# A planned kernel with the orders of its engines exchanged: recurrent attention into a two-expert layer

## The chip, the cores and the metric

One core of a Trainium2 chip runs the program. The metric is the device time of one execution in microseconds; with several runs, their median.

## The reference

The first half is a recurrence over 768 steps for 4 batches of 8 heads of 40 dimensions. Each head keeps a 40x40 state C, a vector n and a maximum m:

```python
m_new = np.maximum(f + m, i)
f_stab, i_stab = np.exp(f + m - m_new), np.exp(i - m_new)
C = f_stab * C + i_stab * np.einsum('bhd,bhe->bhde', vt, kt)
n = f_stab * n + i_stab * kt
y = sigmoid(o_gate) * (C q) / np.maximum(np.abs(n . q), 1.0)
```

Its output, 3072 rows of 320 numbers, goes into a layer of 8 experts with top-1 choice: the logits are `x @ w_gate + modality_bias[modality_id]`, the chosen expert computes `relu(x @ w1[e]) @ w2[e]` (320 to 1024 and back to 320), scaled by the softmax weight of the choice.

## The kernel before, in words

Two parts run interleaved on one core. The **attention part** treats 24 chunks of 128 rows. The first 22 use states that change little (light chunks): states of the first batches are made from k, v and gate weights (`states`, L1890 to L1937), then each light chunk is one product of q with the state. Chunks 0 to 9 take it in full precision (L2042), chunks 10 to 21 as a product of a high and a low half in half precision (L2056); the split of q is done by ACT (the high half, L2049) and DVE (the low half, L2050). The last two chunks of work are special passes with scores (L2146) and values (L2161), for which POOL adds a mask to a sum of gates and takes an offset off (L2150, L2152). After a pair of chunks, `token_rows` divides and gates the rows (DVE L2071 to L2078), POOL or DVE multiplies (L2084, L2086, L2094), ACT rounds to half precision (L2087, L2096), DVE makes the low half (L2089, L2098), and POOL scatters the rows to a table in DRAM, sorted by modality (L2105). A sigmoid of the gates is ACT's L2022; ACT's L2023 is a check of them whose sum (`junk`) is read by the verdict at the end alone.

The **expert part** has 14 tiles of rows, eight for expert A and six for expert B (the stream is A0, A1, A2, B0, B1, A3, ...). For the first three tiles rows are selected on PE by products with selection matrices (L2232 to L2239) and copied by ACT (L2245 to L2249); later ones are loaded from the table (L2200). ACT copies the third part of a tile's columns to where PE needs them in two steps (L2323, L2324: `xt<-xt`). Logits are PE's L2272 and DVE's L2277 to L2293. The first layer is PE's L2344 with its tails L2352, ACT and DVE split the result into two halves (`hh` L2332, `hl` L2333), the second layer is PE's L2403 in groups of four products, ACT scales (L2416) and POOL scatters the result (L2418). Expert weights are loaded in eight pieces for each expert through staging tiles; ACT (L2015) and DVE (L2016) split each piece. One row that fits no tile (`odd_row`) is computed on DVE, with two products on PE (L2443, L2475).

The **order** isn't written in the code as it reads. `still_arm` adds 1126 steps to a `Plan`, each with its engine, an estimated duration and its dependencies. `Plan.run` takes a text, `ORDER` (L1595), two characters for each step, and splits it into one sequence for each engine: 305 steps of PE, 443 of DVE, 200 of ACT, 79 of POOL and 99 of SP, which issues transfers. It walks the sequences by the plan's own estimates to one order in which all instructions are emitted; every engine then runs its own in that order. Three things are derived from the planned times: `gaps` puts fill matmuls of zeros (L2602) into planned gaps of PE in the first 60 us; a GpSimd transfer is made to wait for the DVE step planned ahead of it; and a GpSimd product for the last DVE step of the kind that works within SBUF alone:

```python
flat = [k[a] * len(self.DIGITS) + k[b] for a, b in zip(text[::2], text[1::2])]
...
self.seq = {e: [i for i in flat if ts[i]["eng"] == e] for e in self.ENGINES}
...
order = plan.run(ORDER)
fills = plan.gaps(["M0", "O1", "O0", "Y0", "Y1", "H0", "H1", "H2"], 0.25, 60.0, "zz")
```

Of the kernel before, what the change touches and what calls it, by code (L numbers as in the profile page):

```python
# [1594 lines left out]
ORDER = (  # L1595
    "#:#;#7#W#X#Y$($'$>$=$z$y$L&3&4$N$P&K&L$T$b$c$e%k%l%m%n%,%o%-$h%/%1%t%u%v%w%x%}%~%5'6&#&$&%&&&i&j&k&n&o&r&s&v&w&z&{&|&}&~"
    "'#'(')'*'+','-%^(;(<(=(@(A(D'Q&/'N(E(H(I(L(M(N(O(P(Q(T(U(V(W'v(X(Y'y&[).)/)0)3)4)7)8);)<(i(l)?)@)A)B)C)D)G)H)I)J)K)L'b*4"
    ")V*5*6*9*:)Y*=*>*A)o*B*E)r*F*G*H*I*J*M*N*O*P*Q*R*g*h(,+4*i*l*m*p*q,9*t*u*x+7({*y*z*{*|,>,C*}+$+%+&+'+(+),H*%+W+X+[*W+_+b"
    "+e+f+i+l+o+r+s+t+u+v+w+z+{+|+}+~,#,&,',(,),*,+,.,/,0+F,1,X,2,3,y,z,}-$-'-*,h-+-.-1-Z-4-7-8-9-:-;-<-?-@-A-B-C-D-G-H-I-J-K"
    '-L-O-P-Q-R-S-T.B.C.F.I-r.L.O.P.S.V.Y.].^._.`.a.b.e.f.g.h.i.j.m.n.o.p.q.r.u.v.w.x.y.z/$/%/&/)/*/-/./1/2/5/6/7/8.7/9/:/=/>'  # L1600
    "/?/@/A/B.<#)#|#}#*#+#<#.#9#2#1#3#F#4#=#K#?#>#N#A#G#@#B#T#U'H#H#V#Z#[#I#]#C#D#J$O%0%.#L$&$*$d$.$K#M$)$-$+$,$@$/$D$?$C$A$1"
    "$B$2%$${%#$|$5$}$M$6$G$~$H#R&9&5&:$R&6&7#d&F$U#g%'$f&8%(#s&R#j%q#m&N$V%3$i&M#p'5$W&Q#v#y$X%s%|%z'8$Z&O$[$_'M$`$]$j$k$l%6"
    "%7#6$a&=&>%8&P%N&q&u&m&y$r$s%9&U&V%E%H%?%K%@$n'%%A%;$o%W$p'>$t%_%`'P%Z%a(?%Q'S'R'V%b'T$q'U$^%T'W(C(G(K'u'Z%h'[&0'x%i%j(h"
    "'z&]&^%d%<%=%e%>'~&_&`%f'{'|(#&b'}%g)2(k):)6&f(m'G)>(n(o(&&g&h(')U(r)X(q(p)Z'c)_)n'd(u(v)`'e)[)]'f)^)q*@*8'l*<*D)c)d)t&c"
    "&d&e+3)s)w'h'm'n)x)u)v+<+8){)|'i'j(-(.'k(/*k+6*o(0,=+=(|+9(}(~*w+:)#)%+;)&*s(2,G(6)'(3(7,I(8,J,K,M)(*&,L)))*+@+A*',N+Z(4"
    '*X)++a+^*(*)*+,Q*,*Y*Z,R+h+d*/+k+n(5*0*1+q(b+G+H+I*[,|-#+J-&*^,Y%+*-+L*.,Z,i*_*`,[,]*b*c*a,_,`,a-)*d-[,b-3---0,c,j+M-6,k'
    ",l+N+O-](c-^'_+P+Q+R-_-a,d(d,n,o-b-c(e)g,r,e-e,p'I-l-m'J'K,s,t-n,U-h-i-f-g-o-p-q.E-s-{-d.K-v.H,q-t-u.R(f.N-w-x.U.[.$.X-j"
    ".%.&.'.(.).*.+.,-k.-.:-y-z.../.0.1.2.3.4.5/,.6/0.;/(/4.=###5#S$%#z#8#E#^#_#`$;&E$0$4$w$F&+#c$Q$S#f%&#r$g&C#i%p#l#o%2#u%r"
    "%4#x%{%y'7$Y'L#{&<%M&'&p$m&l&t%D&x&T%V%G%J%:'$'O$<(9(:'=$x%Y'&(>'.%P'3(B%S%c&,(F(J't'Y'w(g&D'4),(R)-'r's(Z)1(j)5)9(%(`&a"
    ")=)T,<)W*2)R)E*3)m(t)k)M*7)p*;*?*C'g)b,7+2+0*f*e*K)z*j(a+5+S*n*r*S#(+T*v,F(1*~+V+?)$+U+Y)S+*+]+`+c**,P+g+j+m+p+x,x,$,,.>"  # L1610
    ",u,w,v,~,{)l-%,4*]+1-(,8.A+K-/,^.?-,-2-5-=-`.@-E,m.~-M.D-U.J.G.M.Q.T.W.Z.c/#.k.s.{/'/+///3.8/;/C#/#,#~#-#P#O#0$3$E%%$I$8"
    "#Q$7%)$J&;%*&?&S&@&W&X&1&('X''']'^,:'/($,;(S((()(s([(w)a(x)f)e)y)F)})N,D,E+>*L*T+B,O)~+C,S+#,T+y++,-,%+,,5->-V-|-F-N.d.l"
    ".t.|-W.}.9/</D#$#%#&#'$9$:$u$v$#&)&*#a#b&A$$#e#q&B#h#k#n#t&-#w&G'0%B%F%L%I%C%U'9'1%[&H&I%X%O'2':';&.'<&J%R'o'p'E(]&Y%]'q"
    "'F'?(^)O(_)P'A)Q'@'`)h'B,A&Z)j'C)i,6+/+-+.(*,B'D(y(+'a,?,@*#(z*U&2+E+D,V,W,f-X*V-Y,g*$-}-~.#"
)
SMALL = dict(tok=NC, u=NC, lo=NC, hi=NC, mod=NC, u25=NHALF, erev=E, mb=NMOD * E, wg=3 * E, tok2=6, cmask=FT)

# [1141 lines left out]
```

## Time and profile before

| | |
|---|---|
| median of 3 runs | 205.23 us (205.13 to 205.27) |
| profiled execution, its own time | 207.16 us |
| its span, first to last instruction | 205.4 us |
| mean granted clock of PE | 0.99 |
| HBM read, written | 23.13 MB, 8.75 MB |

A row of a timeline tells start, duration, engine, line, operation, output and inputs, shape and count (consecutive alike instructions are one row), and in brackets how long the engine had been idle and what released it. PE's rows overlap, since its matmuls are pipelined: what one costs is read from the start of the next.

### The profile page before, as it was taken

How to read it: one execution, taken by the hardware profiler on the slowest of the kernel's cores; microseconds unless marked ns; L12 is line 12 of the kernel's file. 1: busy time of each engine (PE TensorE's matmuls, PEld its weight loads, DVE VectorE, ACT ScalarE, POOL GpSimd, SP SyncE). 2: the span in 40 equal slices, each digit the busy share in tenths (PEclk: the TensorE clock that was granted, in tenths of full speed). 3: DMA queues.
4: the chain of work that ended last, by engine and by line, in shares of the span. 5: the costliest groups of instructions: out<-in, count | busy, mean ns of one | idle time of the engine just before them, and what ended most of it. 6: DMA issues, size and time to landing. Idle time of an engine off the chain costs nothing.

```text
span 205.4 us, 4934 instructions
## 1 busy us (share of the span) xinstructions
PE 195.7 (95%) x1850; PEld 136.0 (66%) x1850; DVE 136.1 (66%) x451; ACT 108.4 (53%) x212; POOL 83.0 (40%) x85
## 2 busy tenths in 40 slices
...
GB/s 182 370 330 392 369 398 220 306 327 238 319 345 260 311 386 190 134 68 176 103 52 99 79 150 190 6 0 32 35 64 0 33 112 389 142 64 20 2 40 34
DMA packets 29548, 35.77 MB, mean 174 GB/s; under 512 B 19421, under 2 KB 21151, under 8 KB 29263
## 3 DMA queue, kind: packets, MB, share of 16 engines
...
q0 software_dynamic: 2416, 8.13, 11.6%
q8 instruction: 15, 0.25, 0.5%
...
HBM read 23.13 MB, written 8.75 MB: 155 GB/s over the span
## 4 chain that ended last, share of the span: by engine, by line
PE 80%; DVE 8%; ACT 4%; issue 3%; POOL 1%; POOLq 0%; ACTq 0%
PE O L2403 35%; PE H L2344 20%; PE H L2352 7%; PE O L2344 6%; PE M L2272 2%; PE M L2602 2%; DVE qst L2050 1%; PE Y L2056 1%; DVE xr L2078 1%; PE Y L2161 1%; PE Y L2146 1%; PE O L2232 1%; ACT qst L2049 1%; ACT junk L2023 1%; PE Y L2042 1%
## 5 line engine op out<-in xcount | busy, mean ns | idle before, releaser
L2418 POOL DMA_INDIRECT out<-ob,ois x25 | 28.2, 1129 | 59.4 <-ACT ob L2416 19.3
L2403 PEld LDWEIGHTS <-hh 128*128 128x128 f16 (+1 forms) x400 | 37.7, 98 | 15.4 <-issue 0.4
L2105 POOL DMA_INDIRECT x_s<-rows,pos_i x24 | 28.5, 1186 | 26.0 <-issue 6.8
L2333 DVE SCALAR_TENSOR_TENSOR hl<-H,hh 128x512 f16<-128x512 f32 (+2 forms) x40 | 25.0, 646 | 18.1 <-ACT hh L2332 17.7
L2332 ACT ACTIVATE hh<-H 128x512 f16<-128x512 f32 (+2 forms) x40 | 22.0, 563 | 28.0 <-PE H L2344 15.9
L2416 ACT ACTIVATE ob<-O,zs 128x320 f32<-128x320 f32 x24 | 12.6, 524 | 30.1 <-PE O L2403 20.7
L2403 PE MATMUL O<-w2hA,hh 128*128 128x320 f16 (+1 forms) x104 | 27.8, 299 | 0.0
L2403 PE MATMUL O<-w2lA,hh 128*128 128x320 f16 (+1 forms) x104 | 27.8, 299 | 0.0
L2403 PE MATMUL O<-w2hB,hh 128*128 128x320 f16 x96 | 26.5, 299 | 0.0
L2403 PE MATMUL O<-w2lB,hh 128*128 128x320 f16 x96 | 26.5, 299 | 0.0
L2344 PE MATMUL H<-xt,w1hA 128*128 128x512 f16 (+3 forms) x128 | 24.5, 295 | 0.0
L2403 PEld LDWEIGHTS <-hl 128*128 128x128 f16 (+1 forms) x200 | 18.9, 98 | 7.8 <-issue 0.7
L2344 PE MATMUL H<-xt,w1hB 128*128 128x256 f16 (+1 forms) x120 | 23.4, 294 | 0.0
L2344 PEld LDWEIGHTS <-w1hA 128*128 128x128 f16 x160 | 13.7, 98 | 8.3 <-issue 2.1
L2344 PEld LDWEIGHTS <-w1hB 128*128 128x128 f16 x160 | 14.8, 98 | 6.2 <-issue 1.9
L2344 PE MATMUL H<-xt,w1lA 128*128 128x512 f16 (+3 forms) x64 | 18.1, 294 | 0.0
L2344 PE MATMUL H<-xt,w1lB 128*128 128x256 f16 (+1 forms) x60 | 17.6, 294 | 0.0
L2094 POOL TENSOR_TENSOR xr<-xr,ab 128x640 f32<-128x640 f32 x11 | 14.0, 1272 | 5.1 <-DVE rows L2098 1.9
L2403 PE MATMUL O<-w2hA,hl 128*128 128x320 f16 (+1 forms) x104 | 15.7, 299 | 0.0
L2050 DVE SCALAR_TENSOR_TENSOR qst<-qg,qst 40x1024 f16<-40x1024 f32 x12 | 15.3, 1271 | 0.3 <-ACT qst L2049 0.3
L2403 PE MATMUL O<-w2hB,hl 128*128 128x320 f16 x96 | 15.2, 299 | 0.0
L2078 DVE SCALAR_TENSOR_TENSOR xr<-og,Y 128x320 f32<-128x320 f32 x24 | 11.5, 479 | 5.3 <-ACT rows L2096 2.5
...
## 6 DMA issues: line engine op xcount, KB each, us to landing
...
```

Source lines behind the costliest of these rows:

```text
L2050: two(H * P, lambda: v.scalar_tensor_tensor(qst[j][0:D], qf[j][0:D], QSC, qst[j][0:D], ALU.mult, ALU.subtract), r=[f"qf{j}"], w=[f"qh{j}"])
L2078: dve(320, lambda h=h: v.scalar_tensor_tensor(x4[:, h], og[k][:, h].rearrange("p (h d) -> p h d", h=H), 1.0, y4[h][:, :, 0:D], ALU.add, AL ...
L2094: on(640, lambda: by.tensor_tensor(x3, x3, ab.rearrange("p c h o -> p (c h) o").broadcast_to([P, 2 * H, D]), ALU.mult), r=abk, w=xk)
L2105: ins = g_.indirect_dma_start(out=x_s[:, :], out_offset=bass.IndirectOffsetOnAxis(ap=pos_i[:, c:c + 1].bitcast(U32), axis=0), in_=rows[:, ...
L2272: t_.matmul(M0[0:n, 16 * h:16 * h + 16], lhsT=s["x"][:, b, P * h:P * h + n], rhs=wgr[:, b % 3].rearrange("p a e -> p (a e)"), start=(h == ...
L2332: act(len(f) * n, lambda: s_.activation(hh[:, sl, 0:n], hp3, AF.Relu), r=[nb], w=[f"hh{p}"])
L2333: dve(len(f) * n, lambda: v.scalar_tensor_tensor(hl[:, sl, 0:n], hp3, 0.0, hh[:, sl, 0:n], ALU.max, ALU.subtract), r=[nb, f"hh{p}"], w=[f" ...
L2344: t_.matmul(dst, lhsT=w[:, i, ws], rhs=two_x(xb), start=(first and b == 0 and q == 0), stop=(last and b == 1 and q == 2), skip_group_check ...
L2352: t_.matmul(dst, lhsT=w[rs, place(f)[0], 2 * T:WP], rhs=two_x(xs[r], rs), start=(f in fresh and q == 0), stop=(f in last and q == 2), skip ...
L2403: t_.matmul(op[p0:p0 + nr, 0:DM], lhsT=t[:, at[f], o_:o_ + nr], rhs=w[:, f], start=(i < ways), stop=(i >= 24 - ways), skip_group_check=True)
L2416: act(DM + 80, lambda op=op, o=o, qc=qc, nr=nr: s_.mul(obs[o][0:nr], op[0:nr, 0:DM], facs[0:nr, qc:qc + 1]), r=[no, f"fac{m_}"], w=[f"ob{o}"])
L2418: swdma(164, lambda o=o, qc=qc, nr=nr: disjoint("outf", g_.indirect_dma_start(out=out[:, :], out_offset=bass.IndirectOffsetOnAxis(ap=ois[0 ...
```

## The change

Only the text `ORDER` is replaced. The steps, their instructions, their dependencies and all the code stay. Since the five sequences are other ones, so are the one order in which instructions are emitted, the fills, and the DVE steps for which POOL's transfers and products wait.

```diff
@@ -1593,25 +1593,25 @@
 ORDER = (
-    "#:#;#7#W#X#Y$($'$>$=$z$y$L&3&4$N$P&K&L$T$b$c$e%k%l%m%n%,%o%-$h%/%1%t%u%v%w%x%}%~%5'6&#&$&%&&&i&j&k&n&o&r&s&v&w&z&{&|&}&~"
-    "'#'(')'*'+','-%^(;(<(=(@(A(D'Q&/'N(E(H(I(L(M(N(O(P(Q(T(U(V(W'v(X(Y'y&[).)/)0)3)4)7)8);)<(i(l)?)@)A)B)C)D)G)H)I)J)K)L'b*4"
-    ")V*5*6*9*:)Y*=*>*A)o*B*E)r*F*G*H*I*J*M*N*O*P*Q*R*g*h(,+4*i*l*m*p*q,9*t*u*x+7({*y*z*{*|,>,C*}+$+%+&+'+(+),H*%+W+X+[*W+_+b"
...
-    ".t.|-W.}.9/</D#$#%#&#'$9$:$u$v$#&)&*#a#b&A$$#e#q&B#h#k#n#t&-#w&G'0%B%F%L%I%C%U'9'1%[&H&I%X%O'2':';&.'<&J%R'o'p'E(]&Y%]'q"
-    "'F'?(^)O(_)P'A)Q'@'`)h'B,A&Z)j'C)i,6+/+-+.(*,B'D(y(+'a,?,@*#(z*U&2+E+D,V,W,f-X*V-Y,g*$-}-~.#"
+    "#:#;#7#W#X#Y$($'$>$=$z$y&4&3$L$N$P&L&K$b$c$e$T%k%l%m%n%o%,%-%/%1$h%t%u%v%w%x%}%~&#'6%5&$&%&&&i&j&k&n&o&r&s&v&w&z&{&|&}&~"
+    "'#'(')'*'+','-%^(;(<(=(@(A(D'N'Q(E(H(I(L(M(N(O'v&/(P(Q(T(U(V(W(X(Y'y&[).)/)0)3)4)7(l)8(i);)<)?)@)A)B)C)D)G)H)I)J)V)Y)K)L"
+    "'b*4*5*6*9*:*=*>)r*A)o*B*E*F*G*H*I*J*M*N*O*P*Q*R(,*g*h*i*l*m*p*q+7*t+4*u({,9*x*y,>*z*{*|*}+$+%+&+',C+(+),H*%+W+X+[*W+_+b"
...
+    ".d.}.t.9.|/</D#$#%$##&#'$9$:$u$v&)$$&*&A#a#e#b#n#h#k&-#q#t&B&G#w%B'0%F%C%I%X'9'1%L%[%R%U&I%O&H&J'<':';'2'o'p(]%]&Y'?(^&."
+    "'q)O'B'A(_)P'@)Q)h&Z'`'E)i'C'F)j+/'a+-,6(*'D,A+.&2(z(y,B,@,?*#*U(+*$+D,g*V,V+E-Y-X,W,f-}-~.#"
 )
```

Decoded, the fewest steps that have to be taken out and put back to turn one sequence into the other are 28 of PE's 305, 235 of DVE's 443, 97 of ACT's 200, 31 of POOL's 79 and 45 of SP's 99. The fills (columns of zeros) become:

| ahead of | before | after |
|---|---|---|
| the counts, L1950 | 2699 | 3444 |
| the turn of the gate weights, L1879 | 1135 | 818 |
| the first states, L1911 | 772 | 772 |
| light chunk 1 | 836 | 808 |
| light chunk 3 | 364 | 251 |
| light chunk 5 | 1163 | 2319 |
| light chunks 6 and 7 | 1394 | 260 |
| select of tile 0, chunk 2 | 0 | 332 |
| logits of tile 0 | 0 | 302 |

The moves that the text below speaks of (places in the sequence of the step's own engine):

| engine | step | move |
|---|---|---|
| PE | light chunks 7 and 6, L2042 | ahead of all selects of tile 0, 7 before 6 |
| PE | light chunk 9 before 8; logits of tile 0 | logits behind the selects of tile 1 |
| PE | values of light chunk 12, L2056 | 7 places earlier |
| PE | values of chunks 15, 14, L2056 | 4 and 1 earlier, into the first layer of tile 4, 15 first |
| PE | values of chunks 16, 17, 19, 21 | 4, 8, 4, 5 earlier |
| PE | values of chunk 20; special scores and values, pair 0; scores, pair 1 | 7 later; 4 later and 3 earlier; 5 later |
| DVE | low state half, L1937 | 32 earlier, behind the rows of pair 0 |
| DVE | low half of q, L2050, of chunk 14 | 8 later, next ahead of the logits of tile 4 |
| DVE | L2050 of chunks 15, 16, 17 | 3 earlier, 8 earlier, 2 later |
| ACT | checks L2023 of pairs 0, 1 | 30 and 41 earlier |
| ACT | split of piece 0 of A's weights, L2015; pieces 1 and 4 | 4 later; 1 and 6 earlier; now 1, 0, 4 |
| ACT | last copy of tile 0, L2249 | 4 later, behind those three splits |
| ACT | rounding of pair 4, L2096 | 6 earlier |
| ACT | copies of tile 3, L2323, L2324; split of piece 6 of B | 2 and 3 later; 13 later, behind the copies |
| ACT | high half of q, L2049, of chunk 11, of chunk 15 | 7 later, behind the copies; 5 earlier |
| POOL | product of pair 4, L2094 | ahead of the scatter of chunk 6 |
| POOL | special mask sum L2150, pair 0 | 8 later |
| SP | store of zero rows, L2121 | 6 earlier, ahead of the first loads of q and the gates |
| SP | loads of A's pieces 0, 1 and 4 | 3 later, 1 and 4 earlier: now 1, 0, 4 |
| SP | loads of q of chunks 14, 15 | 2 and 4 earlier |

## Rows read from the trace of the kernel before

**Rows 1.** The page, part 1: busy time of each engine.

```profile
PE 195.7 (95%) x1850; PEld 136.0 (66%) x1850; DVE 136.1 (66%) x451; ACT 108.4 (53%) x212; POOL 83.0 (40%) x85
```

**Rows 2.** The page, part 4: the chain that ended last, shares by engine.

```profile
PE 80%; DVE 8%; ACT 4%; issue 3%; POOL 1%; POOLq 0%; ACTq 0%
```

**Rows 3.** The table of stages: length, then PE, PEld, DVE, ACT, POOL busy; clock, DMA share, GB/s.

```profile
10.00:20.00 10.00, 9.87 (x124) 8.43 (x123) 9.39 (x38) 7.31 (x14) 5.20 (x5) 1.00 1.01 361
...
100.00:150.00 50.00, 50.00 (x390) 28.42 (x388) 26.89 (x88) 21.77 (x49) 15.01 (x16) 1.00 0.28 67
```

**Rows 4.** PE's waits: who waited for whom, in total, times, longest.

```profile
PE Y L2056 <- DVE qst L2050: 0.6, 1, 0.6
```

**Rows 5.** Timeline of PE, the start: start, duration, line, operation, count.

```profile
1.07 2.43 PE L2602 MATMUL M<-zz 128*128 128x512 bf16 x6 [1.07 <-DVE zz L1832]
...
10.91 0.66 PE L2602 MATMUL M<-zz 128*128 128x512 bf16 x3
11.50 1.61 PE L2042 MATMUL Y<-S,qg 120*64 120x123 f32 x18
...
19.31 0.29 PE L2344 MATMUL H<-xt,w1hA 128*128 128x128 f16 x2
```

**Rows 6.** Timeline of ACT, the start.

```profile
15.51 0.74 ACT L2015 ACTIVATE w1hA<-stage 128x640 f16<-128x640 f32 x1 [0.23 <-DMA stage<-in_w1s]
...
16.76 0.37 ACT L2249 CAST xt<-O 128x256 f16<-128x256 f32 x1
17.46 0.74 ACT L2015 ACTIVATE w1hA<-stage 128x640 f16<-128x640 f32 x1 [0.33 <-DMA stage<-in_w1s]
```

**Rows 7.** Timeline of DVE, the start.

```profile
17.70 0.53 DVE L1937 SCALAR_TENSOR_TENSOR S<-S,S 120x369 f16<-120x369 f32 x1
```

**Rows 8.** Timeline of PE, the tails of the fourth tile and of a later one.

```profile
41.30 0.60 PE L2352 MATMUL H<-xt,w1hB 64*128 64x256 f16 x2
...
43.37 0.39 PE L2344 MATMUL H<-xt,w1hB 128*128 128x256 f16 x2
...
71.94 0.39 PE L2352 MATMUL H<-xt,w1hA 64*128 64x256 f16 x4
...
73.35 0.39 PE L2344 MATMUL H<-xt,w1hA 128*128 128x256 f16 x2
```

**Rows 9.** Timeline of ACT ahead of those tails.

```profile
36.23 0.72 ACT L2096 CAST rows<-xr 128x640 f16<-128x640 f32 x1 [0.99 <-POOL xr L2094]
...
40.25 0.82 ACT L2023 ACTIVATE junk<-og,nglo 128x640 bf16<-128x640 f32 x1
...
41.61 0.40 ACT L2324 COPY xt<-xt 64x256 f16<-64x256 f16 x1
```

**Rows 10.** Timeline of PE at the values of chunks 14 and 15.

```profile
62.12 0.36 PE L2056 MATMUL Y<-Sst,qst 120*128 120x41 f16 x8
63.08 0.37 PE L2056 MATMUL Y<-Sst,qst 120*128 120x41 f16 x8 [0.60 <-DVE qst L2050]
63.29 0.30 PE L2403 MATMUL O<-w2hB,hh 128*128 128x320 f16 x1
```

**Rows 11.** Timeline of DVE ahead of them.

```profile
56.85 0.19 DVE L2277 TENSOR_REDUCE lg<-M 128x16 f32<-128x32 f32 x1 [1.26 <-PE M L2272]
...
57.69 1.07 DVE L2289 SCALAR_TENSOR_TENSOR ois<-zs 128x1 int32<-128x1 f32 x1
...
60.42 0.10 DVE L2289 SCALAR_TENSOR_TENSOR ois<-zs 128x2 int32<-128x2 f32 x1
...
61.03 1.99 DVE L2050 SCALAR_TENSOR_TENSOR qst<-qg,qst 40x1024 f16<-40x1024 f32 x1
```

**Rows 12.** Line 2050 alone: all twelve, least, median and longest ns.

```profile
L2050 DVE SCALAR_TENSOR_TENSOR qst<-qg,qst x12: 1154/1210/1987, 29.7 to 89.9; 40x1024 f16<-40x1024 f32 x12
```

**Rows 13.** Timeline of POOL beside those steps.

```profile
57.48 1.27 POOL L2150 TENSOR_TENSOR kws<-S,cst 128x512 f32<-128x512 f32 x1 [1.11 <-PE M L2272]
...
60.69 1.25 POOL L2094 TENSOR_TENSOR xr<-xr,ab 128x640 f32<-128x640 f32 x1 [0.65 <-DVE ois L2289]
```

More of the change, by code (lines that the diff above doesn't have):

```diff
@@ L1595 @@
 ORDER = (
-    "#:#;#7#W#X#Y$($'$>$=$z$y$L&3&4$N$P&K&L$T$b$c$e%k%l%m%n%,%o%-$h%/%1%t%u%v%w%x%}%~%5'6&#&$&%&&&i&j&k&n&o&r&s&v&w&z&{&|&}&~"
-    "'#'(')'*'+','-%^(;(<(=(@(A(D'Q&/'N(E(H(I(L(M(N(O(P(Q(T(U(V(W'v(X(Y'y&[).)/)0)3)4)7)8);)<(i(l)?)@)A)B)C)D)G)H)I)J)K)L'b*4"
-    ")V*5*6*9*:)Y*=*>*A)o*B*E)r*F*G*H*I*J*M*N*O*P*Q*R*g*h(,+4*i*l*m*p*q,9*t*u*x+7({*y*z*{*|,>,C*}+$+%+&+'+(+),H*%+W+X+[*W+_+b"
-    "+e+f+i+l+o+r+s+t+u+v+w+z+{+|+}+~,#,&,',(,),*,+,.,/,0+F,1,X,2,3,y,z,}-$-'-*,h-+-.-1-Z-4-7-8-9-:-;-<-?-@-A-B-C-D-G-H-I-J-K"
@@ L1600 @@
[L1600 to L1611, printed above, removed]
@@ L1612 @@
-    "#Q$7%)$J&;%*&?&S&@&W&X&1&('X''']'^,:'/($,;(S((()(s([(w)a(x)f)e)y)F)})N,D,E+>*L*T+B,O)~+C,S+#,T+y++,-,%+,,5->-V-|-F-N.d.l"
-    ".t.|-W.}.9/</D#$#%#&#'$9$:$u$v$#&)&*#a#b&A$$#e#q&B#h#k#n#t&-#w&G'0%B%F%L%I%C%U'9'1%[&H&I%X%O'2':';&.'<&J%R'o'p'E(]&Y%]'q"
-    "'F'?(^)O(_)P'A)Q'@'`)h'B,A&Z)j'C)i,6+/+-+.(*,B'D(y(+'a,?,@*#(z*U&2+E+D,V,W,f-X*V-Y,g*$-}-~.#"
+    "#:#;#7#W#X#Y$($'$>$=$z$y&4&3$L$N$P&L&K$b$c$e$T%k%l%m%n%o%,%-%/%1$h%t%u%v%w%x%}%~&#'6%5&$&%&&&i&j&k&n&o&r&s&v&w&z&{&|&}&~"
+    "'#'(')'*'+','-%^(;(<(=(@(A(D'N'Q(E(H(I(L(M(N(O'v&/(P(Q(T(U(V(W(X(Y'y&[).)/)0)3)4)7(l)8(i);)<)?)@)A)B)C)D)G)H)I)J)V)Y)K)L"
@@ new lines @@
+    "'b*4*5*6*9*:*=*>)r*A)o*B*E*F*G*H*I*J*M*N*O*P*Q*R(,*g*h*i*l*m*p*q+7*t+4*u({,9*x*y,>*z*{*|*}+$+%+&+',C+(+),H*%+W+X+[*W+_+b"
+    "+e+f+i+l+o+r+s+t+u+v+w+z+{+|+}+~,#,&+F,',(,),*,+,.,/,0,1,2,3,y,z,}-$,X-'-*,h-+-.-1-4-7-8-9-:-;-Z-<-?-@-A-B-C-D-G-H-I-J-K"
+    '-L-O-P-Q-R-S-T.B.C-r.F.I.L.O.P.S.V.Y.].^._.`.a.b.e.f.g.h.i.j.m.n.o.p.q.r.u.v.w.x.y.z/$/%/&/)/*/-/..7/1/2/5/6/7/8/9/:/=/>'
+    '/?/@/A/B.<#)#1#|#*#}#+#F#2#9#3#G#4#R#.#=#<#>#K#H#?#A#T#B#I#U#V#@#Z#C#[#]#J#D#L$M$d$K$O#M#N$.$*$)$-&F$+%.$,$&$/$@$?$D$C$A'
```

11 lines of the change are left out of this document (added).

## The prediction

> **What bounds the kernel now.** I read the page first: PE is busy for 195.7 us of a span of 205.4 [rows 1], and the chain that ended last lies on PE for 80% of the span [rows 2]. The edit adds and removes no instruction but the fill matmuls of the first 20 us, so it can only gain or lose where PE waits. The table of stages says where that can be: in the ten microseconds from 10 us the 16 DMA engines, PE and DVE are all full (DMA share 1.01, DVE 9.39 of 10 us), while from 100 us PE is busy for 50.00 of 50.00 us and DVE for 26.89, ACT for 21.77, POOL for 15.01 [rows 3]. Late orders of the other engines have room to spare, early ones have none. What is left is the start (the first expert product stands at 19.31 [rows 5]) and the holes in PE after it. The list of waits names one of over half a microsecond, 0.6 us for the step L2050 [rows 4]. A second is in no list: the tails (L2352) of the fourth tile take from 41.30 to 43.37, 2.07 us, the same group of a later tile from 71.94 to 73.35, 1.41 us [rows 8]. So 0.66 us is lost there, spread over matmuls that look busy.
>
> **The start.** Two fills ahead of the first small products change from 2,699 to 3,444 columns and from 1,135 to 818, together 428 more. Six matmuls with 2,699 columns take 2.43 us [rows 5], 0.90 ns a column, so 0.39 us; nothing covers it, as the turn of the gate weights comes right behind. Some is regained at the next fills, which fall mostly after the granted clock has risen from half to full. The fill ahead of light(5) grows from 1,163 columns to 2,319; the old one takes 0.66 us from 10.91, and the product starts at 11.50 [rows 5], so 1,156 more columns end near 12.1. That costs nothing extra, since the DVE steps that light(5) reads also come later: the low state half (L1937, 0.53 us at 17.70 [rows 7]) is moved in among them, ahead of 32 other steps, and the other movements there cancel. The select of the first tile then ends about 0.35 us later.
>
> What decides is when ACT has copied the first tile and split the weights. In the old order A's piece 0 is split at 15.51, the last copy of tile 0 (L2249) starts at 16.76 and piece 1 is split at 17.46, both pieces on landing [rows 6]. Now piece 1 is loaded ahead of piece 0, and pieces 1, 0 and 4 are all split ahead of that copy. The same bytes stand ahead of the second landing as before, so it stays near 17.46, and piece 4, 328 KB at the 361 GB/s of the stage [rows 3], lands 0.91 us later, at 18.37. Its split (0.74) and the copy (0.37) end at 19.48, against 17.13 before. The two sigmoid checks (L2023, 0.82 each by [rows 9]) that move into the first 15 us mostly fill ACT's waits for landings. With the hand-over and PE's own delay I take +0.55 us for the first expert product. Bounds: zero, if the copy is still in time (it had 2.18 us to 19.31), and one more late load, +0.91. The prefill store moved ahead of the first q and gate loads on SP's queue is within that; it costs light(1) perhaps 0.2.
>
> **The tails of the fourth tile.** They need two copies on ACT, the last at 41.61 (0.40) [rows 9]. Ahead of them ACT waited 0.99 us for POOL's product (the row at 36.23), and did a check (0.82, at 40.25) which nobody waits for before the end [rows 9]. Now POOL does that product before the scatter of chunk 6, ACT has the check behind it by 20 us, and the qst step L2049 stands behind the copies. But splits of B's weights and the check of pair 2 come ahead of them, so ACT's work ahead of the last copy grows by 0.97 us. The wait of 0.99, work that no longer ends late, and piece 6's split put behind them make it come out near 40.9. I take the whole 0.66 us; the bounds are 0 and 0.66.
>
> **The values of chunks 14 and 15.** Eight matmuls take 0.21 us (63.08 to 63.29), so the first eight end at 62.33 and PE loses 0.75 us until 63.08 [rows 10]. It waits for DVE's L2050 of chunk 15, at 61.03 and 1.99 us long [rows 11], where the median is 1.21 [rows 12]. DVE had waited 1.26 us for the logits at 56.85, and a step of 0.10 us took 1.07 at 57.69 [rows 11], beside POOL's mask sum (L2150) of 1.27 us at 57.48; the long L2050 began beside another, at 60.69 [rows 13]. The new order puts the L2050 of chunk 14 right ahead of the logits, so it fills that wait; L2150 goes eight places back, to about 75 us; and L2050 of chunk 15 has 1.39 us less work ahead of it. So it should end at 61.03 + 1.21 − 1.39 − 1.26 − 0.97 = 58.6. On PE these eight matmuls (chunk 15, now ahead of chunk 14) move forward by 2.33 us of work and want it at 62.33 − 2.33 = 60.0. That leaves 1.4 us: −0.75 us. ACT's half of chunk 15 has 4.09 us less work ahead of it and is not in the way. The lower bound on the gain is none.
>
> The two slowed steps show that a step of POOL and one of DVE can hold each other up for nearly a whole instruction. The Trainium skill ("SBUF — State Buffer", the section on SBUF's two separate sides) states this as an exclusive lock on a shared port pair, the loser blocked for the whole instruction; by that rule L2150 does not lose its price when it is moved, but takes it to its new neighbour. The trace agrees as to the block: 1.07 us in place of 0.10 [rows 11], beside 1.27 [rows 13].
>
> **The rest.** Values of chunks 16, 17, 19 and 21 go forward on PE by 4, 8, 4 and 5 places, 12 and 20 by 7 forward and 7 back, with their DVE steps moved by less; scores and values of a special pass get only two groups of products between them. Logits, the odd row's product, drains and about half of the DVE, ACT and SP places move where there is slack. Each forward move may make a wait: none at best, about one of 0.75 us (the size seen [rows 10]) at worst. I take 0.15, a fifth of it. After PE's last product nothing changes.
>
> **Sum.** +0.55 − 0.66 − 0.75 + 0.15 = −0.71 us. The profiled run took 207.16 us, 1.93 above the median of 205.23, about 1.7 of it outside its span; both kernels carry that, so I take the difference to the median: **204.5 us**. Within 0.2%, 0.41 us, a measurement of this kernel can't tell a change from none.
>
> **Rivals.**
> Slower: *light(15) is too early.* If DVE gains only the 1.39 us of work moved behind, not the waits and blocked steps, then PE, 2.33 us earlier, waits 0.94 us longer instead of 0.75 less: +0.55 − 0.66 + 0.94 = +0.83, 206.1 us. For it: DVE is full there, and another order puts other waits in. Against: 1.26 + 0.97 + 0.78 = 3.0 us of its time there is waiting and blocking that the order itself makes. It decides if L2050 of chunk 15 ends behind 60.0 us. Chance 0.20.
> *The copies of the fourth tile come no earlier*, because ACT's extra 0.97 us takes what the waits gave: −0.71 + 0.66 gives 205.2. Chance 0.16.
> *The block moves with L2150*: beside a DVE step that PE reads at its new place it costs what [rows 11] show on L2050, 1.99 − 1.21 = 0.78: −0.71 + 0.78, 205.3. For it: both slow rows. Against: beyond 65 us few DVE steps are awaited. Chance 0.08.
> *The start is no later*, because the copy's old slack of 2.18 us still holds: −0.71 − 0.55, 204.0. Chance 0.14.
> *The changed order changes nothing that matters*, PE being filled either way: 205.2. Chance 0.02.
>
> **The numbers.** The forecast has 0.40, with 203.8 to 204.8 as its own range. Faster: 0.40 + 0.14 = 0.54. Same: 0.16 + 0.08 + 0.02 = 0.26. Slower: 0.20. The range runs from both gains with no loss, 0 − 0.66 − 0.75 = −1.41, a little below which is 203.7, to the slower rival, 206.1.
>
> **What would show it.** Right: the first expert product at 19.7 to 20.0; the fourth tile's tails in 1.4 us; no wait of PE for L2050 of chunk 15, which ends by 60; the end 0.7 us earlier. Wrong: a wait of over 0.3 us for a copy or L2050 between 40 and 100 us, a first expert product behind 20.3, or a tail of the fourth tile that still takes 2 us.

## The result and the profile after

The new kernel takes 207.56 us (median of 6 runs, 206.63 to 208.69), the kernel before in the same comparison 205.42 us (205.13 to 206.36): ratio 1.010, 95% interval 1.0064 to 1.0136. Forecast were 204.5 us and a range that ended at 206.1. The profiled execution took 207.7 us with a span of 206.0, so it is a typical one. The one of the kernel before was not: 207.16 us against a median of 205.23. (All ratios below are of fast runs: slow ones, which lay over 1.5% above a kernel's fastest or had a lower granted clock, are left out, five of n_checks' twelve and two or fewer of any other.) A second profile of the same kernel (b_again, below) took 206.19 us with a span of 204.4 and stands for it in this table, which gives where PE's steps start in the three timelines:

| PE step | before, first profile | before again | after | after less before again |
|---|---|---|---|---|
| light chunk 1 | 7.42 | 7.09 | 7.62 | +0.53 |
| light chunk 3 | 9.47 | 9.11 | 10.18 | +1.07 |
| light chunk 5 | 11.50 | 11.49 | 12.82 | +1.33 |
| first tile, first product | 19.31 | 19.53 | 20.45 | +0.92 |
| first tile, second step of the first layer | 19.66 | 19.88 | 21.34 | +1.46 |
| first tile, second layer, fourth group | 27.73 | 27.95 | 29.71 | +1.76 |
| fourth tile, behind the tails | 43.37 | 43.19 | 44.69 | +1.50 |
| fifth tile, second layer | 63.29 | 62.34 | 63.70 | +1.36 |
| verdict | 198.03 | 197.10 | 198.58 | +1.48 |

The last column sums up PE in these two executions: all is lost by 30 us, a little comes back, and from the fifth tile on the difference hardly changes (+1.36 to +1.48). Against the first profile light(1) and light(3) are only 0.20 and 0.71 later. Their columns hold some 0.3 us that is no step's doing: in b_again PE ran the small products ahead of them (L1911) in 0.27 us each from 5.5 us on, in the other two in 0.41 until 7 us. From light(5) on both profiles of before agree. The whole 2.1 us between the medians is not in this pair, which differs by 1.5. Part 4 of the page of the new kernel, and of b_again's:

```profile
PE 84%; DVE 4%; DMA 3%; ACT 3%; issue 2%; POOL 1%; SPq 1%; POOLq 0%; DVEq 0%
```

```profile
PE 77%; DVE 7%; DMA 6%; ACT 3%; issue 3%; POOL 1%; SPq 1%; POOLq 0%
```

PE is as busy as before [rows 1]. The chain has the load `og<-in_ogl` in it, for 3%, which is not in that of [rows 2]; but it is in b_again's too, for as much, so it is no mark of the new order. The start on PE, where the rows of before are [rows 5]; in brackets the idle time ahead of a row and what ended it:

```profile
1.07 3.05 PE L2602 MATMUL M<-zz 128*128 128x512 bf16 x7 [1.07 <-DVE zz L1832]
...
10.18 1.57 PE L2042 MATMUL Y<-S,qg 120*128 120x123 f32 x12 [0.99 <-DVE ab L2071]
...
20.45 0.27 PE L2344 MATMUL H<-xt,w1hA 128*128 128x128 f16 x2
21.10 0.23 PE L2344 MATMUL H<-xt,w1lA 128*128 128x128 f16 x1 [0.38 <-DVE w1lA L2016]
```

The first fill has seven matmuls in 3.05 us in place of six in 2.43, and the step behind the two fills (L1879) starts at 4.79, where it stood at 4.53 and in b_again at 4.44: 0.26 to 0.35 us later. Light(3) waits for DVE. The first tile's first product comes without a wait, late because PE's own work ahead of it is late (light(5) at 12.82); its next step, on the low weight halves, waits for DVE. On ACT [rows 6]:

```profile
8.80 0.74 ACT L2022 ACTIVATE og<-og 128x640 f32<-128x640 f32 x1 [0.95 <-DMA og<-in_ogl]
...
10.60 0.81 ACT L2023 ACTIVATE junk<-og,nglo 128x640 bf16<-128x640 f32 x1
...
11.41 0.72 ACT L2022 ACTIVATE og<-og 128x640 f32<-128x640 f32 x1
...
19.61 0.37 ACT L2249 CAST xt<-O 128x256 f16<-128x256 f32 x1 [0.45 <-DVE zs L2248]
...
26.93 0.73 ACT L2015 ACTIVATE w2hA<-stage 128x640 f16<-128x640 f32 x1
27.67 1.28 ACT L1826 ACT_TABLE_LOAD   x1
28.97 0.38 ACT L2332 ACTIVATE hh<-H 128x256 f16<-128x256 f32 x1
29.25 0.37 ACT L2249 CAST xt<-O 128x256 f16<-128x256 f32 x1
```

The sigmoid of the first gates (L2022 at 8.80) has waited for its load. The check of them (L2023) stands ahead of the second sigmoid. The last copy of the first tile (L2249 at 19.61) ends at 19.98, behind a wait for DVE and 0.5 us later than forecast, but PE reaches the tile at 20.45 and is not held by it. And at 27.67 stands what the prediction never mentions: a load of ACT's function table, 1.28 us, which in the kernel before stood at 91.9 us, moved by 89 places, ahead of the last copy of the third tile. PE's logits wait for that copy:

```profile
29.67 0.18 PE L2272 MATMUL M<-wgr,xt 128*128 128x16 f16 x1 [0.30 <-ACT xt L2249]
```

DVE, right ahead of the low weight halves that the first tile waits for (L2016):

```profile
17.88 1.42 DVE L2075 TENSOR_SCALAR ab<-ab 128x16 f32<-128x16 f32 x1
...
19.50 1.54 DVE L2016 SCALAR_TENSOR_TENSOR w1lA<-stage,w1hA 128x640 f16<-128x640 f32 x2
```

L2075, a step on 16 columns, takes 1.42 us. It is the step of pair 3 and reads nothing of what POOL makes at the same time:

```profile
16.50 1.45 POOL L2105 DMA_INDIRECT x_s<-rows,pos_i  x1 [1.39 <-ACT og L2022]
17.98 1.27 POOL L2094 TENSOR_TENSOR xr<-xr,ab 128x640 f32<-128x640 f32 x1
```

The two holes that were forecast to close are closed. The tails of the fourth tile take 1.42 us (43.27 to 44.69, before 2.07 [rows 8]), and the values of chunk 15, now ahead of those of chunk 14, wait for nothing [rows 10]:

```profile
43.27 0.39 PE L2352 MATMUL H<-xt,w1hB 64*128 64x256 f16 x4
...
44.69 0.39 PE L2344 MATMUL H<-xt,w1hB 128*128 128x256 f16 x2
...
61.33 0.36 PE L2056 MATMUL Y<-Sst,qst 120*128 120x41 f16 x8
...
62.19 0.36 PE L2056 MATMUL Y<-Sst,qst 120*128 120x41 f16 x8
```

The tails close for another reason than was forecast. ACT's last copy for them starts 1.0 us later than before (41.61 [rows 9]), not earlier, and is in time because PE comes later still:

```profile
42.61 0.40 ACT L2324 COPY xt<-xt 64x256 f16<-64x256 f16 x1
```

On DVE the L2050 of chunk 14 fills the wait ahead of the logits (L2277), and that of chunk 15 ends at 59.30 (58.15 + 1.15), before 63.02 [rows 11]:

```profile
55.91 1.21 DVE L2050 SCALAR_TENSOR_TENSOR qst<-qg,qst 40x1024 f16<-40x1024 f32 x1
57.05 0.17 DVE L2277 TENSOR_REDUCE lg<-M 128x16 f32<-128x32 f32 x1
...
58.15 1.15 DVE L2050 SCALAR_TENSOR_TENSOR qst<-qg,qst 40x1024 f16<-40x1024 f32 x1
```

POOL's mask sum, L2150, at its new place at 76 us holds a DVE step of 16 columns, L2075 (they end at 77.39 and 77.43), and PE shows no wait behind it. POOL, then DVE:

```profile
74.89 1.19 POOL L2105 DMA_INDIRECT x_s<-rows,pos_i  x1 [1.76 <-DVE ab L2071]
76.10 1.29 POOL L2150 TENSOR_TENSOR kws<-S,cst 128x512 f32<-128x512 f32 x1
```

```profile
75.47 1.96 DVE L2075 TENSOR_SCALAR ab<-ab 128x16 f32<-128x16 f32 x1
```

The transfers have changed too. The table of stages, for the kernel before again and for the new one (the two last columns are the share of the DMA engines and GB/s):

```profile
25.00:30.00 5.00, 5.00 (x59) 3.84 (x54) 5.00 (x15) 3.72 (x10) 4.53 (x4) 1.00 1.03 400
30.00:35.00 5.00, 5.00 (x71) 4.51 (x71) 4.51 (x18) 3.65 (x9) 1.78 (x3) 1.00 0.70 227
```

```profile
25.00:30.00 5.00, 4.70 (x65) 3.56 (x63) 5.00 (x15) 4.70 (x9) 3.82 (x3) 1.00 0.72 277
30.00:35.00 5.00, 5.00 (x66) 4.30 (x64) 4.64 (x18) 3.99 (x9) 2.20 (x3) 1.00 0.88 226
```

From 25 to 35 us the new kernel moves (277 + 226) x 5 = 2.5 MB, the old (400 + 227) x 5 = 3.1 MB. SP's issues in the new kernel show why:

```profile
23.80 0.33 SPq L2014 DMA_DIRECT2D stage<-in_w1s  x1
29.19 0.33 SPq L2014 DMA_DIRECT2D stage<-in_w  x1
31.76 0.36 SPq L1816 DMA_DIRECT2D qg<-in_q  x1
32.35 0.34 SPq L2014 DMA_DIRECT2D stage<-in_w1s  x1
```

From 24.13 to 29.19 SP issues nothing. Its next step is the load of piece 7 of B's weights, moved 7 places earlier, and its staging tile is free only when DVE has split piece 7 of A's. Behind it on the queue stand q of chunk 11 and pieces 3 and 6, whose own tiles were free at 25.1 and 27.1. (Ahead of q, SP waits again, until 31.32, for the states that it stores.)

### The profile page after: what moved, and what is told of

The parts are those of the page before. It is cut to its first block, busy times and chain, and to the rows that moved or that the text cites. A ratio compares the mean times of both kernels' runs of the same rounds, so it can differ in the third digit from the quotient of the medians.

```text
span 206.0 us, 4946 instructions
## 1 busy us (share of the span) xinstructions
PE 195.7 (95%) x1852; PEld 135.7 (66%) x1852; DVE 138.7 (67%) x451; ACT 108.8 (53%) x212; POOL 81.5 (40%) x85
## 4 chain that ended last, share of the span: by engine, by line
PE 84%; DVE 4%; DMA 3%; ACT 3%; issue 2%; POOL 1%; SPq 1%; POOLq 0%; DVEq 0%
PE O L2403 38%; PE H L2344 24%; PE H L2352 8%; PE O L2344 8%; DMA og<-in_ogl 3%; PE M L2272 1%; PE Y L2056 1%; PE Y L2161 1%; PE Y L2146 1%; DVE xr L2078 1%; DVE w1lA L2016 1%; ACT og L2022 1%; PE O L2232 1%; ACT L1826 1%; ACT w2hA L2015 0%
## 5 line engine op out<-in xcount | busy, mean ns | idle before, releaser
L2418 POOL DMA_INDIRECT out<-ob,ois x25 | 25.4, 1017 | 58.0 <-issue 28.3
L2105 POOL DMA_INDIRECT x_s<-rows,pos_i x24 | 30.1, 1252 | 28.7 <-DVE hl L2333 3.3
L2094 POOL TENSOR_TENSOR xr<-xr,ab 128x640 f32<-128x640 f32 x11 | 13.9, 1268 | 8.6 <-DVE qst L2050 7.0
L2050 DVE SCALAR_TENSOR_TENSOR qst<-qg,qst 40x1024 f16<-40x1024 f32 x12 | 14.5, 1218 | 0.3 <-ACT qst L2049 0.3
L2049 ACT ACTIVATE qst<-qg 120x1024 f16<-120x1024 f32 x12 | 12.6, 1052 | 0.2
```

What stands on the lines that cost most here:

```text
L2049: act(H * P, lambda: s_.mul(qst[j][0:120], qf[j][0:120], QSC), r=[f"qf{j}"], w=[f"qh{j}"])
L2050: two(H * P, lambda: v.scalar_tensor_tensor(qst[j][0:D], qf[j][0:D], QSC, qst[j][0:D], ALU.mult, ALU.subtract), r=[f"qf{j}"], w=[f"qh{j}"])
L2094: on(640, lambda: by.tensor_tensor(x3, x3, ab.rearrange("p c h o -> p (c h) o").broadcast_to([P, 2 * H, D]), ALU.mult), r=abk, w=xk)
L2105: ins = g_.indirect_dma_start(out=x_s[:, :], out_offset=bass.IndirectOffsetOnAxis(ap=pos_i[:, c:c + 1].bitcast(U32), axis=0), in_=rows[:, ...
L2418: swdma(164, lambda o=o, qc=qc, nr=nr: disjoint("outf", g_.indirect_dma_start(out=out[:, :], out_offset=bass.IndirectOffsetOnAxis(ap=ois[0 ...
```

## The experiments

Each kernel was timed in alternation with the kernel before on the same chip. In some series the kernel before itself took 205.4 us, in others 207.3 (the chip numbered 8 stands by both), so only ratios are compared. A diff shows the sequence of an engine, decoded, where a step is moved; order text and fills follow from that. "Fills" kept means that the column counts of the fills are written down instead of planned.

**The kernel before, again** (b_again; nothing changed).

> The kernel before itself, to see whether the two holes on which the forecast's gains rest belong to it or to its one profiled execution (207.16 us, 1.9 us above the median). Theory 'the holes are its own': tails of the fourth tile take 2.07 us again, PE waits 0.6 us for L2050 of chunk 15, span about 205.4. Rival 'they were of that execution': span about 203.5, tails 1.4 us, no wait for L2050, and then nothing in the new order can be gained there.

Measured: 205.74 us, ratio 1.0016 (0.9996 to 1.0035), span 204.4. The timelines of PE and DVE:

```profile
41.52 0.65 PE L2352 MATMUL H<-xt,w1hB 64*128 64x256 f16 x4
...
61.93 0.56 PE L2056 MATMUL Y<-Sst,qst 120*128 120x41 f16 x16
```

```profile
56.20 1.32 DVE L2289 SCALAR_TENSOR_TENSOR ois<-zs 128x1 int32<-128x1 f32 x1
...
60.04 1.72 DVE L2050 SCALAR_TENSOR_TENSOR qst<-qg,qst 40x1024 f16<-40x1024 f32 x1 [0.18 <-ACT qst L2049]
```

The tails keep a part of their hole (41.52 to 43.19, 1.67 us). The hole ahead of the values of chunks 14 and 15 is gone: all sixteen matmuls run in one piece. DVE is blocked as before (L2289 1.32, L2050 1.72), but came to L2050 a microsecond earlier. So both theories are half right: of the 1.41 us that the prediction meant to win, some 0.25 were there to be won in this execution. Even this one, at 206.19 us, lies above the median of its series.

**Start and rest exchanged** (old_start: the old sequences for the steps that the old plan starts ahead of the first expert product, the new ones behind; new_start: the other way round).

```diff
-        self.seq = {e: [i for i in flat if ts[i]["eng"] == e] for e in self.ENGINES}
+        self.seq = {e: [i for i in first[e] if i in S] + [i for i in rest[e] if i not in S] for e in self.ENGINES}
```

> The old sequences for the 163 steps that the old plan starts ahead of the first expert product, then the new sequences for all others. Theory 'the start alone makes it slower' (first expert product 1.5 us later in the new kernel): it takes 1.5 us off the new kernel, about 206.1, first expert product near 19.4. Rival 'the loss is spread over the stretch behind': the start is the old one and the time stays above 207.

> The other way round: the new sequences for the 170 steps that the new plan starts ahead of the first expert product, then the old sequences. Theory 'the start': 1.5 us above the kernel before, about 206.9, first expert product behind 20.4. Rival 'behind the start': within 0.4 us of the kernel before.

Measured: 209.80 us, ratio 1.0226 (1.0188 to 1.0264), and 210.88 us, 1.0281 (1.0249 to 1.0313). Neither says which theory holds. 209.80 does lie above the 207 of the rival, but the planner had seen a gap at the seam and filled it, with a fill of 8,229 columns and with three of 7,952 together, over 3 us on PE. So the same with the seven or nine fills of their start alone (p_old_start, p_new_start):

```diff
-    fills = plan.gaps(["M0", "O1", "O0", "Y0", "Y1", "H0", "H1", "H2"], 0.25, 60.0, "zz")
+    fills = {23: ("M0", 2699), 20: ("M0", 1135), 52: ("O1", 772), 96: ("Y0", 836), 118: ("O1", 364), 177: ("M0", 1163), 289: ("M0", 1394)}
```

> As old_start, but with the seven old fills alone (8,363 columns): in old_start the planner had put a fill of 8,229 columns ahead of the select of the third tile, and PE's steps behind it stand 3.3 us later. Theory 'the loss is the start': 209.8 - 3.4 = 206.4 or a little less, as the table load of ACT at 28 us is still in it (0.45 us); against the kernel before +0.2 to +0.8 us. Rival 'the new order behind the start is slower in itself': above 207.

> As new_start, but with the nine new fills alone (9,306 columns). Theory 'the loss is the start': the first expert product 1.1 to 1.5 us later than in the kernel before and all of it kept to the end: 206.5 to 206.9. Rival: within 0.4 us of the kernel before, the old order behind the start absorbing it.

Measured: 1.0177 (1.0151 to 1.0203) and 1.0194 (1.0149 to 1.0239). The gap was a real one. PE's longest wait in p_old_start, from the list of waits:

```profile
PE O L2232 <- ACT xt L2245: 2.8, 1, 2.8
```

Steps that ACT and DVE do for the third tile stand in the other part and come late at the seam. Behind PE's waits there (until 24.49; in p_new_start 1.75 us until 28.17) the granted clock is 0.50, that is 1.2 GHz, from 25.9 to 29.2 us (28.6 to 31.9); in old_start and new_start, with the large fills, it is 1.00 all through. A part of these losses is the clock, then. The four runs say nothing on the question: two orders can't be cut across the middle of a stage.

**The table load back** (a_table_back; the new kernel, ACT's sequence).

```diff
-  ..., hh2 tile 0, split A7, table load L1826, hh3 tile 0, copy L2249 tile 2, ...
+  ..., hh2 tile 0, split A7, hh3 tile 0, copy L2249 tile 2, ..., ob tile 5, table load L1826, ...
```

> The new kernel with one step moved: the load of ACT's function table (L1826, 1.28 us, at 27.67) goes back to its old place behind the special pass, near 92 us. Theory 'the table load delays the copy L2249 of the third tile, and PE waits for it': 0.4 to 0.5 us faster than the new kernel, about 207.1, and no hole behind the logits of the third tile. Rival 'that wait would come anyway, from DVE or the next ACT step': no change.

Measured: 208.92 us, ratio 1.0171 (1.0129 to 1.0213), if anything slower than the new kernel itself, whose interval touches it. The hole in the logits is gone, and others have come: the tails of the fourth tile take 1.79 us again, and PE waits for a transfer of states, in PE's timeline:

```profile
46.86 0.35 PE L2056 MATMUL Y<-Sst,qst 120*128 120x41 f16 x8 [0.58 <-DMA Sst<-S_d]
```

PE was 1.1 us further than in the new kernel at 40 us, and lost it again by 56 us. That was the first sign of a second limit, the transfers.

**Two small undoings of the start** (a_fill_cut, a_store_back; the new kernel, fills kept).

```diff
-177: ("O1", 2319)
+177: ("O1", 1163)
```

> The new kernel with the fill ahead of light(5) cut from 2,319 to its old 1,163 columns. Theory 'light(5) waits for DVE's gated rows (they end at 12.77, light(5) starts at 12.82)': no change, within 0.2 us of 207.56. Rival 'the fill holds PE': 0.3 to 0.5 us faster.

```diff
-  SP: gs, kv0, store L2121, q0, og0, q1, og1, q2, og2, ...
+  SP: gs, kv0, q0, og0, q1, og1, q2, og2, store L2121, ...
```

> The new kernel, fills as they are, with one transfer moved: the store of zero rows (L2121) goes back behind the first eight loads on SP. Theory 'the store delays the first gate load, so the sigmoid, the gated rows and light(3)': the first sigmoid ends 0.6 to 1.0 us earlier, the time falls by 0.5 to 0.9 us, to about 206.8. Rival 'ACT's check and the low state half ahead of the second pair hold light(5) anyway': less than 0.2 us.

Measured: 1.0099 (1.0065 to 1.0133), no change against 1.010, as expected; and 1.0079 (1.0051 to 1.0107). The second is not clear of 1.010 either. In its profile, of an execution 1.2% above the kernel's median, the first tile's second step starts at 20.85 in place of 21.34, though light(5) comes 1.0 us earlier; DVE's L2075 takes 1.94 us there.

**Both limits, one by one and together** (a_start, a_sp, a_all; the new kernel, fills kept). a_start puts back five steps; a_sp reorders SP; a_all does both.

```diff
-  SP:   kv0, store L2121, q0, og0, ...
+  SP:   kv0, q0, og0, ..., og2, store L2121, ...
-  ACT:  check pair 0, sigmoid pair 1, ..., check pair 1, ..., split A7, table load, ...
+  ACT:  sigmoid pair 1, ..., Sh of state 2, check pair 0, ..., rounding pair 4, check pair 1, ..., ob tile 5, table load, ...
-  POOL: product pair 1, scatter chunk 1, product pair 2, ...
+  POOL: product pair 1, product pair 2, scatter chunk 1, ...
```

```diff
-  SP:   B1, B0, B2, B7, S_d2, q11, B3, tile 3, B5, B6, ...
+  SP:   B1, B0, B2, B3, B6, B7, q11, S_d2, tile 3, B5, ...
```

> The new kernel with five steps back at their old neighbours: the store of zero rows behind the first loads (SP), the checks of pairs 0 and 1 and the table load later (ACT), POOL's product of pair 2 ahead of the first scatter, where it no longer runs beside DVE's L2075 and the low weight halves. Fills are the new kernel's. Theory 'two limits' (a late start, and a transfer queue that runs dry from 25 to 35 us): the first expert product comes about 1 us earlier, but waits for transfers and copies between 40 and 65 us take most of it back: the ratio to the kernel before stays 1.007 to 1.010. Rival 'the start alone': 1.002 to 1.005.

> The new kernel with SP's loads of B's pieces 3, 6 and 7 and of q of chunk 11 put directly behind that of piece 2, so that the wait for the staging tile of piece 7 (5 us on SP, to 29.19) no longer stands ahead of transfers that could go. Theory 'two limits': the DMA share of 25 to 30 us rises from 0.72 to 0.9 or more, but the time hardly moves, 0 to 0.4 us, since PE is late from the start already: ratio 1.008 to 1.010. Rival 'the transfers alone': 1 us or more faster, ratio below 1.005.

> Both groups of moves together. Theory 'two limits': now the start's gain is kept, more than the sum of the two runs beside it: 1.2 to 1.8 us faster than the new kernel, ratio 1.001 to 1.004. Rival 'something else behind the start': above 1.006.

Measured: a_start 207.06 us, 1.0069 (1.0042 to 1.0097), runs from 205.53 to 207.31; a_sp 207.19 us, 1.0091 (1.0057 to 1.0125); a_all 205.63 us, 1.0000 (0.9982 to 1.0019), runs from 205.09 to 205.93. In a_sp the transfers no longer stop:

```profile
25.00:30.00 5.00, 4.70 (x60) 3.41 (x58) 4.78 (x16) 4.70 (x10) 4.31 (x4) 1.00 1.05 381
30.00:35.00 5.00, 5.00 (x69) 4.46 (x67) 4.87 (x19) 3.88 (x8) 2.21 (x3) 1.00 1.06 288
```

Neither alone is clear of the new kernel's own 1.0064 to 1.0136, both together give all of the loss back: theory "two limits". (The forecasts of 1.007 to 1.010 for a_start and of 1.001 to 1.004 for a_all were just missed, both on the fast side.) That a_all is faster than a_start is clear, in one series; by which wait of PE the start repaired alone still loses is not shown. That it comes where transfers are late is inferred from the spread of its runs, which a_all does not have, and from the wait in a_table_back; a_start's one profile is that of its fastest run (205.53 us) and shows no hole. In a_all the tails do what the prediction said, with a PE that is in time. ACT's last copy for them, then PE:

```profile
40.60 0.40 ACT L2324 COPY xt<-xt 64x256 f16<-64x256 f16 x1
```

```profile
41.27 0.39 PE L2352 MATMUL H<-xt,w1hB 64*128 64x256 f16 x4
...
42.69 0.39 PE L2344 MATMUL H<-xt,w1hB 128*128 128x256 f16 x2
```

**The store alone, on the kernel before** (b_store; the diff of a_store_back turned round).

> The kernel before with the store of zero rows alone moved ahead of the first loads of q and the gates, as the new order has it; fills are the old ones. Theory 'the store delays the first gate load': the first sigmoid and light(3) come 0.6 to 1.0 us later and the time rises by 0.4 to 0.9 us, ratio 1.002 to 1.004. Rival 'within the slack', as the prediction had it: below 1.001.

Measured: 206.08 us, ratio 1.0040 (1.0017 to 1.0062), beside 1.0016 (0.9996 to 1.0035) for nothing changed. The first sigmoid ends at 9.25 (before again 8.54), light(3) starts at 9.83 (9.11). In its profile the first tile is on time all the same (19.84, 19.88); so by what path the time rises is not shown.

**One of the five left in** (n_pool, n_checks, n_table: a_all with one step as in the new order), and **the rest of the old start** (a_best: a_all with the first fill at 2,699, the fill ahead of light(5) at 1,163 columns, and L1937 behind the rows of pair 2).

```diff
 n_pool, POOL:
-  product pair 1, product pair 2, scatter chunk 1, ...
+  product pair 1, scatter chunk 1, product pair 2, ...
```

> The repaired kernel a_all with POOL's product of pair 2 behind the first scatter again, as the new order has it. Theory 'the product then runs beside DVE's L2075 and holds it up for over a microsecond, right ahead of the low weight halves that the first expert product waits for': L2075 1.4 us or more, the first expert product 0.4 to 0.9 us later, ratio 1.002 to 1.005 (a_all 1.000). Rival 'it was only late because the rest was': below 1.001.

> a_all with the two sigmoid checks of pairs 0 and 1 on ACT as early as in the new order. Theory 'the first check stands ahead of the sigmoid of pair 1': light(5) 0.3 to 0.6 us later, ratio 1.001 to 1.003. Rival, the prediction's: they fill ACT's waits and cost nothing, below 1.001.

> a_all with the load of ACT's function table ahead of the last copy of the third tile, as in the new order. Theory: that copy comes late, PE waits 0.4 us in the logits of the third tile, ratio 1.001 to 1.003. Rival: below 1.001, the wait being made by the late start.

> a_all with three things of the old start more: first fill 2,699 columns, fill ahead of light(5) 1,163, and the low state half (L1937) behind the rows of pair 2 instead of pair 0. Theory 'light(1) and light(5) are 0.3 to 0.45 us later than in the kernel before through these': both come as early as there, ratio 0.997 to 0.999. Rival 'weights and copies of the first tile set its first product now': 0.999 to 1.001.

Measured in one series: n_pool 1.0118 (1.0081 to 1.0155), n_checks 1.0023 (0.9997 to 1.0049), n_table 1.0056 (1.0031 to 1.0081), a_best 0.9998 (0.9973 to 1.0024). So n_pool, which differs from a_all by the one place of POOL's product, is as slow as the new kernel; the table load costs more than was expected; the checks stay unclear. a_best does not beat the kernel before. In n_table PE waits for the copy behind the table load:

```profile
PE M L2272 <- ACT xt L2249: 0.8, 1, 0.8
```

In n_pool DVE, POOL and PE show what happens:

```profile
16.20 1.94 DVE L2075 TENSOR_SCALAR ab<-ab 128x16 f32<-128x16 f32 x1
```

```profile
15.62 1.18 POOL L2105 DMA_INDIRECT x_s<-rows,pos_i  x1 [2.18 <-DVE rows L2098]
16.84 1.27 POOL L2094 TENSOR_TENSOR xr<-xr,ab 128x640 f32<-128x640 f32 x1
```

```profile
19.96 0.23 PE L2344 MATMUL H<-xt,w1lA 128*128 128x128 f16 x1 [0.75 <-issue]
```

L2075 ends at 18.14, POOL's product at 18.11, and PE comes to the first low weight half 0.75 us late. That is not the whole 1.2%, some 2.4 us. In this profile ACT also waits 2.05 us ahead of a step at 40.31 (L2412) for what the profile calls remote, and PE for ACT behind it. The same wait stands in n_checks' profile (3.19 us, an execution of 210.58 us), which has the product in its old place, so it is not tied to that place; how much of the 1.2% is the product's is open. In a_all the product is further on when DVE arrives:

```profile
16.89 0.40 DVE L2075 TENSOR_SCALAR ab<-ab 128x16 f32<-128x16 f32 x1
```

```profile
16.00 1.26 POOL L2094 TENSOR_TENSOR xr<-xr,ab 128x640 f32<-128x640 f32 x1 [1.87 <-DVE rows L2098]
```

**The two large ones undone alone** (a_two: the new kernel with the POOL step and the four loads on SP as in a_all, store, checks and table load as in the new order), and **the POOL move alone on the kernel before** (b_pool).

```diff
 b_pool, POOL:
-  product pair 1, product pair 2, scatter chunk 2, scatter chunk 1, ...
+  product pair 1, scatter chunk 1, product pair 2, scatter chunk 2, ...
```

> The new kernel with two things undone: POOL's product of pair 2 ahead of the first scatter, and SP's loads of B's pieces in an order without the wait. Store, checks and table load stay as the new order has them. Theory 'these two are the larger part': ratio 1.002 to 1.006, L2075 of pair 2 under 0.5 us. Rival 'all five of the start are needed': 1.007 or more.

> The kernel before with POOL's scatter of chunk 1 moved ahead of its product of pair 2, as the new order has it, and nothing else; fills are the old ones. Theory 'the product then runs beside DVE steps right ahead of the first low weight halves and holds them up': a DVE step between 16 and 19 us takes over 1 us, the first expert product 0.5 to 1 us later, ratio 1.003 to 1.008. Rival 'only the new DVE order is hit': below 1.002.

Measured: a_two 208.22 us where the kernel before took 207.25, 1.0031 (1.0007 to 1.0055); b_pool 207.94 us, 1.0043 (1.0019 to 1.0066). The POOL step and the four loads of SP, undone together, take some 0.7 of the 1.0% away. In a_two L2075 takes 0.40 us again and the second step starts at 20.56, not 21.34, though light(5) is as late as in the new kernel (12.76, 12.82). (The expectation calls this L2075 that of pair 2; it is pair 3's, beside the product of pair 2.) In b_pool the time is as expected and the path is not: in the old DVE order no step is blocked, and the first tile is on time (19.10). The product itself is late, as the scatter ahead of it waits 3.81 us; ACT's rounding of its rows waits for it, and behind that on ACT stands the copy of the second tile:

```profile
20.29 0.72 ACT L2096 CAST rows<-xr 128x640 f16<-128x640 f32 x1 [2.81 <-POOL xr L2094]
...
21.56 0.46 ACT L2245 CAST xt<-O 128x384 f16<-128x384 f32 x1
```

PE's select of the third tile waits for that copy:

```profile
22.07 0.22 PE L2232 MATMUL O<-sel,rows 128*128 128x128 f16 x1 [1.58 <-ACT xt L2245]
```

## Why the prediction was wrong

**What bounds the kernel** was read rightly: all that happened, happened at the start and in PE's holes, and next to nothing behind 65 us. But "early ones have none" was not carried through: the DVE, POOL and SP moves of the start were taken to cancel.

**The start: mis-sized.** Forecast was +0.55 for the first expert product; it came +0.92 (b_again) to +1.14 (first profile) later, and the second step of that tile, which the prediction did not ask about, +1.46. The fills cost a little less than was forecast (+0.26 to +0.35, forecast +0.39), and cutting the long one changes nothing, as said. Three steps failed. The store ahead of the loads was put at "perhaps 0.2" for light(1); moved alone, in b_store, it moves the sigmoid and light(3) by 0.7 us each. The first tile was argued from ACT's copy and splits, at 19.48 to 19.86; that copy did come late, but the first product was held by PE's own late start, which followed from light(3) and light(5), and the second step by DVE's low halves (21.10), which stand behind L2075. And POOL's scatter ahead of the product of pair 2 was not costed at all: 1.0118 in n_pool against 0.9998 for a_best beside it and 1.0000 for a_all, in another series, which differs by that move alone; 1.0043 in b_pool, where it acts by another path.

The prediction did weigh this mechanism, and at the wrong place. It read from [rows 11] and [rows 13] that a POOL step can hold a DVE step for a whole instruction, and asked it of L2150 alone, one of 31 POOL steps that move. In after, n_pool and a_all alike L2075 ends 0.03 to 0.05 us behind the end of the product (19.30 and 19.25, 18.14 and 18.11, 17.29 and 17.26), whatever time it began. The Trainium skill ("SBUF — State Buffer", the section on SBUF's two separate sides) says that the loser fully blocks; these three rows agree. In every profile with the new order of DVE this L2075 takes 0.40 us where the product stands first and 1.41 to 1.94 where the scatter does.

**The table load: missing.** It is an ACT step of 1.28 us in the trace of before, without inputs or outputs, and so without a row in a reading that goes by tiles. It cost 0.3 us as a wait in the new kernel and +0.30 in the table above (from +1.46 to +1.76), and in n_table 0.56% of the time. Moved back alone, in a_table_back, it gave nothing.

**SP's queue: missing.** The prediction followed A's pieces 0, 1 and 4 and not B's piece 7, ahead of loads that were ready. The loss is not seen as a wait of PE in the new kernel, whose late start hides it; it shows once the start is repaired (a_start 1.0069, a_all 1.0000). This may be why the parts don't add: the four moves tried singly cost 0.4, 1.2, 0.2 (unclear) and 0.6%, more than the 1.0% of all, though the first was tried on the kernel before and the others on a_all, in other series.

**The tails and the values of chunks 14 and 15: wrong in worth, and the tails closed by chance in the new kernel.** For the values the mechanism is right: L2050 of chunk 15 ends at 59.30 where 58.6 was forecast and 60.0 was the limit; and in a_all, where PE is not late, at 57.05, with PE's values at 59.33 and no wait. For the tails it holds in a_all, where ACT's last copy is 1.0 us earlier than before (40.60; 40.9 was forecast). In the new kernel that copy is 1.0 us later (42.61), and the hole is closed only because PE is late too. But both were sized from an execution of 207.16 us. The prediction said that it lay 1.93 us above the median, put about 1.7 of that outside the span, and let "both kernels carry that". But every execution has 1.7 to 1.8 us outside its span (207.16 and 205.4, 206.19 and 204.4, 207.7 and 206.0), so the excess lay inside it, and the holes that were counted could be part of it: b_again's fifth tile stands 0.95 us earlier (63.29, 62.34), and 0.75 of that is the hole of chunk 15, which isn't there. The gain against that execution is 0.25 at the tails (1.67 to 1.42), less than a fifth of the 1.41 counted.

**The rivals.** Two happened, without their price. The copies of the fourth tile came no earlier, yet cost nothing with PE late. The block did move with L2150: at 76.10 it holds L2075 until 77.43, 1.96 us where the median is 0.17; no wait of PE shows behind it. So that rival had the right mechanism, and the block that counted was that of another POOL step. The slower one priced light(15) as too early, 206.1 us; light(15) was in time. "New waits, 0.15" stood for all moves that had not been followed, and there, and in the start, lay the result.
